# Weight preparation of a fused attention and feed-forward kernel: w3 @ w_out first and whole, lo parts by TensorE and ScalarE, attention queued a slot later

## The chip, the core and the metric

The kernel runs on one core of a Trainium2 chip. A core has five engines with a queue of instructions each: TensorE (PE in the profile; its weight loads are PEld), VectorE (DVE), ScalarE (ACT), GpSimd (POOL) and SyncE (SP, which here only issues DMAs). Matmuls write to PSUM, a memory of eight banks of 128 x 512 fp32; everything else is in SBUF. The metric is the device time of one execution in microseconds; lower is better.

## The reference

Random-feature attention over 8 batches of 576 tokens with 8 heads of 64, and then a bilinear feed-forward block over all 4608 tokens:

```python
def phi(x):                        # 128 random features for each head
    proj = einsum('bhsd,md->bhsm', x, omega)
    h = proj - sum(x * x, -1) / 2
    return exp(h - max(h)) / sqrt(m)
q_p, k_p = phi(q * scale), phi(k * scale)
kv  = einsum('bhsm,bhsd->bhmd', k_p, v);  z = sum(k_p, axis=2)
x   = einsum('bhsm,bhmd->bhsd', q_p, kv) / (einsum('bhsm,bhm->bhs', q_p, z) + 1e-6)
a, b = x @ w1, x @ w2              # x: 4608 x 512, w1 and w2: 512 x 1024
out  = ((a * b) @ w3) @ w_out      # w3: 1024 x 1024, w_out: 1024 x 512
```

q, k, v and omega are fp32, the four weights are float64. The result is fp32.

## The kernel before

**Precision.** An fp32 operand is split into two fp16 parts, hi and lo (x times a power of two s, hi = fp16(x s), lo = x s - hi), and a product is three fp16 matmuls: hi hi, hi lo, lo hi (`PASSES`). `split` (line 132) makes hi on ScalarE and lo on VectorE, with one fused multiply and subtract (lines 136 and 139). `power_of_two` and `pow2` find the scales.

**Weights.** The weights lie in HBM as float64. `from_float64` brings 1 MB at a time into the `arena` as pairs of 32-bit words, by a DMA on ScalarE's queue (`fetch`), takes a magnitude on ScalarE (line 451) and puts the fp32 value together in four VectorE operations (lines 457 to 461). There are three raw buffers. w3 and w_out are never used one by one: the kernel forms W = w3 @ w_out (1024 x 512) with fp32 matmuls and splits that. Here it is done in two halves: two loads of w_out (four of its eight row blocks) and four w3 blocks `W`, whose products give half of every sum; later the other two loads of w_out and four more w3 blocks, whose products VectorE adds to the first (line 537). The fp32 values of w_out and w3 are guests in the second half of `w12b`, where later the second halves of w1 and w2 go. `w12_load` brings a half of w1 or w2, with column sums of the magnitudes by a matmul with ones (line 485), and `w12_split` makes its eight fp16 parts; `W_split` makes those of W and the factors that undo the scales.

**Order of the weights.** `ORDER` is a string of 25 steps: `o` a w_out load, `W` a w3 block, `1` and `2` loads of w1 and w2, `a` and `b` their splits, `S` the split of W. `SKEW` staggers a step's five stages (fetch, magnitude, conversion, nothing, product or magnitudes) over four ticks. `PER` says how many ticks a slot of the main program takes.

**Tokens.** There are 36 chunks of 128 tokens, and three slots of the program for each. The k side runs five chunks ahead of the q side (`LEAD`). `step` puts a chunk's work into slots: sums of squares, scale and split of the raw q and k; in the chunk's first slot `q_chunk` and `k_chunk`, that is projections by 24 matmuls each (`qpj`, `kpj`, line 254), the maximum (line 259), the exponential, and the features' hi and lo parts. A q chunk's features then go through two transposing DMAs on SP's queue (`eqT`, line 344). When a batch's k chunks are done, `kv_batch` forms its kv (line 322). Two slots after `q_chunk` comes `q_attend`: the attention matmuls `nu` (line 357) and the division; one slot after that `ready`: `x_turn` splits x and transposes it by DMA into `xT`.

Two PSUM pools: `ps_a` has two buffers of two banks, shared by qpj, kpj, kv and nu; `ps_m` has four banks for everything else.

**Gates and outputs.** `ready` also appends to a queue the chunk's `gate` units (a, b and their product; for the first four chunks one by one with 96 matmuls of 128 columns each, then in pairs with 48 matmuls of 256 columns) and the `project_out` units (24 matmuls of 512 columns) of the group before. In each slot the program takes one unit from the queue, ahead of the slot's other work; a gate unit waits for the split of its half of w1 and w2, an output for `W_split`. From slot 41 on two units are kept back (`RESERVE`, `EAGER`). What is left at the end is run then.

**Who orders.** The slots give each instruction its priority. A planner that knows the dependences and buffers then writes each engine's order, with its own estimate of when operands are ready: an instruction whose operand it believes late is passed by later ones. At run time each engine keeps that order.

## Time and profile before

| | |
|---|---|
| median of three runs | 932.87 us (929.71 to 1192.34) |
| the profiled execution | 932.87 us, its span 931.1 us |
| mean granted TensorE clock | 0.929 of full speed |
| TensorE busy | 809.9 us (87%) |
| VectorE busy | 637.7 us (68%) |
| ScalarE busy | 406.9 us (44%) |
| GpSimd busy | 324.7 us (35%) |
| DMA | 88.42 MB, mean 95 GB/s |

Times are microseconds from the start of the span unless marked ns. In rows of groups stand the line of the kernel, engine, operation, output <- inputs, shapes and count, then busy time and mean ns of one, then the engine's idle time ahead of them and who ended it. Rows in order of time begin with start and duration; [ ] tells the idle time before and who ended it. An fp32 matmul leaves two records. The rows of stretches give length, then each engine's busy time with its count, the granted TensorE clock, the DMA engines' share and GB/s.

### The profile page before, as it was taken

To read this page: it belongs to the slowest core of one execution; us is meant where nothing else is said; L and a number is where in the kernel's file an instruction comes from. 1 tells how busy PE (TensorE), PEld (TensorE's weight loads), DVE (VectorE), ACT (ScalarE), POOL (GpSimd) and SP (SyncE) were. 2 spreads that over 40 slices of the span, in tenths; PEclk is the share of its full clock that TensorE was granted. 3 is DMA by queue.
4 is the path that set the end of the run, shared out by engine and by line. 5 is a ranking of instruction groups with operands and counts; after the bars stand their busy time and mean duration, and the time that the engine had idled before them with its cause. 6 is when DMAs were issued, how large, how long until landed. Compare 5 with 4: busy or idle time off the path is not lost.

```text
span 931.1 us, 20482 instructions
## 1 busy us (share of the span) xinstructions
PE 809.9 (87%) x8593; PEld 598.3 (64%) x8598; DVE 637.7 (68%) x1119; ACT 406.9 (44%) x695; POOL 324.7 (35%) x317
## 2 busy tenths in 40 slices
PE   1964397689996998999989998989899989999998
PEld 1433253577775766777757766767577757777774
DVE  5779789889787478667876787566857875556210
ACT  3587764556435343444344533444354333322111
POOL 0000004232454256433543464343533643423311
PEclk9985599689998799999989998999899989999999
DMA  8445455332444145333432343243423422333200
GB/s 312 163 137 181 136 148 178 83 70 59 92 114 83 43 91 126 92 70 81 114 80 69 80 125 80 65 96 79 115 71 69 69 59 58 74 76 58 46 24 34
DMA packets 142524, 88.42 MB, mean 95 GB/s; under 512 B 116704, under 2 KB 116832, under 8 KB 142432
## 3 DMA queue, kind: packets, MB, share of 16 engines
q1 hardware_dynamic: 134944, 66.15, 30.1%
q10 hardware_dynamic: 7488, 20.97, 6.7%
q8 instruction: 67, 1.10, 0.5%
q14 instruction: 25, 0.20, 0.1%
HBM read 49.35 MB, written 9.44 MB: 63 GB/s over the span
## 4 chain that ended last, share of the span: by engine, by line
PE 45%; DVE 25%; ACT 11%; DMA 10%; issue 5%; POOL 4%; ACTq 0%; DVEq 0%; SPq 0%; another core or an unknown queue 0%; POOLq 0%
PE ab L581 24%; PE o L607 9%; DVE nm L259 5%; PE kvp L322 4%; PE wp L530 4%; DMA eqT<-eq 3%; DMA qraw<-qT 3%; DVE qhl L139 3%; DVE vhl L139 2%; DVE qe L267 2%; POOL eq L277 2%; PE nu L357 2%; DVE ke L267 2%; ACT ke L268 1%; DMA xT<-xhl 1%
## 5 line engine op out<-in xcount | busy, mean ns | idle before, releaser
L581 PE MATMUL ab<-xT,w12b 128*128 128x256 f16 (+1 forms) x3840 | 408.7, 268 | 12.8 <-DMA xT<-xhl 11.4
L581 PEld LDWEIGHTS <-w12b 128*128 128x128 f16 x3840 | 351.4, 101 | 59.4 <-DMA xT<-xhl 6.8
L607 PE MATMUL o<-Wb,arena 128*128 128x512 f16 x864 | 194.4, 379 | 1.3 <-DVE Wb L139 0.8
L595 POOL TENSOR_SCALAR arena<-asb 128x512 f16<-128x512 f32 x72 | 59.7, 829 | 256.4 <-DVE asb L591 249.5
L607 PEld LDWEIGHTS <-arena 128*128 128x128 f16 x864 | 84.4, 100 | 93.9 <-issue 1.4
L277 POOL TENSOR_TENSOR eq<-qe,eq 128x1024 f16<-128x1024 f32 x34 | 73.3, 2157 | 139.7 <-DVE eq L125 139.7
L268 ACT ACTIVATE qe<-qe,ln_e,es 128x1024 f32<-128x1024 f32 x35 | 43.4, 1240 | 149.5 <-DVE qe L267 149.5
L596 POOL TENSOR_TENSOR arena<-asb,arena 128x512 f16<-128x512 f32 x72 | 92.0, 1277 | 6.0
L139 DVE SCALAR_TENSOR_TENSOR qhl<-qraw,s,qhl 128x512 f16<-128x512 f32 x36 | 68.5, 1904 | 28.6 <-ACT qhl L136 28.5
L591 DVE TENSOR_TENSOR asb<-ab,asb 128x512 f32<-128x512 f32 x72 | 49.5, 688 | 55.3 <-PE ab L581 54.9
L277 POOL TENSOR_TENSOR ek<-ke,ek 128x1024 f16<-128x1024 f32 x28 | 61.5, 2195 | 46.6 <-DVE ek L125 45.3
L153 ACT ACTIVATE junk_q<-qraw 128x512 bf16<-128x512 f32 x36 | 22.7, 631 | 125.2 <-DMA qraw<-qT 125.2
L357 PE MATMUL nu<-kv,eqT 128*128 128x65 f16 (+1 forms) x960 | 40.7, 204 | 40.5 <-DMA eqT<-eq 40.0
L357 PEld LDWEIGHTS <-eqT 128*128 128x128 f16 (+1 forms) x960 | 35.6, 107 | 51.6 <-DMA eqT<-eq 45.2
L530 PE MATMUL wp<-w12b 128*128 128x512 f32 x128 | 62.4, 644 | 4.8 <-DVE w12b L461 4.8
L322 PE MATMUL kvp<-vhl,ek 128*128 128x65 f16 x960 | 50.5, 206 | 11.0 <-POOL ek L277 4.7
L603 DVE TENSOR_SCALAR osc<-pt,kap 128x1 f32<-128x1 f32 x36 | 9.6, 272 | 68.8 <-ACT o L611 68.7
L322 PEld LDWEIGHTS <-ek 128*128 128x128 f16 x960 | 41.4, 104 | 22.4 <-POOL ek L277 4.8
L590 ACT ACTIVATE asb<-ab 128x512 f32<-128x512 f32 x72 | 41.8, 580 | 28.2 <-PE ab L581 28.2
L254 PE MATMUL kpj<-om,khl 64*128 64x128 f16 x864 | 34.0, 226 | 21.5 <-ACT khl L136 17.2
L530 PEld LDWEIGHTS wp<-w12b 128*128 128x128 f32 x128 | 25.7, 206 | 35.6 <-issue 29.9
L393 ACT ACTIVATE xhl<-xs,p2r 128x512 f16<-128x512 f32 x36 | 25.8, 718 | 49.3 <-DVE p2r L182 44.3
(120 smaller groups left out, 1037.5 us busy)
## 6 DMA issues: line engine op xcount, KB each, us to landing
kraw<-kT SPq DMA_DIRECT2D x36, 256.0 KB, 3.0
vraw<-v SPq DMA_DIRECT2D x36, 256.0 KB, 3.0
qraw<-qT SPq DMA_DIRECT2D x36, 256.0 KB, 2.6
out<-o SPq DMA_DIRECT2D x36, 256.0 KB, 2.0
arena<-w3T ACTq DMA_DIRECT2D x8, 1024.0 KB, 5.4
arena<-w ACTq DMA_DIRECT2D x8, 1024.0 KB, 5.9
arena<-wo ACTq DMA_DIRECT2D x4, 1024.0 KB, 5.3
eqT<-eq SPq DMA_TRANSPOSE x72, 3.0
```

The lines of the kernel that those rows point to most:

```text
L139: nc.vector.scalar_tensor_tensor(lo, src, s, hi, ALU.mult, ALU.subtract)
L259: nc.vector.tensor_reduce(nm, pj, AX.X, ALU.max, negate=True)
L268: nc.scalar.activation(e, e, AF.Exp, scale=es, bias=ln_e)
L277: (nc.vector if lo == "d" else nc.gpsimd).tensor_tensor(t[:, 1], e, t[:, 0], ALU.subtract)
L322: nc.tensor.matmul(ps[:, h // 4, h % 4], ek[c][r0:r1, x, place(h)], vhl[c][r0:r1, y, h], start=n == 0, stop=n == len(mm) - 1,)
L357: nc.tensor.matmul(nu[r0:r1, h // 4, h % 4], t[:, x, place(h), r0:r1], kvs[b][:, y, h], start=n == 0, stop=n == 2,)
L530: nc.tensor.matmul(ps, w[:, j, k * P : (k + 1) * P], guest[:, j], start=j == 0, stop=j == HALF - 1)
L581: nc.tensor.matmul(ps[:, k], w12[m][i][cc][:, a, r * P : (r + 1) * P], x[:, b, cc, off : off + T], start=j == 0, stop=j == len(mm) - 1,)
L591: nc.vector.tensor_tensor(asb, ab[1], asb, ALU.mult)
L595: nc.gpsimd.tensor_scalar(h[:, 0], asb, 1.0, 1.0, ALU.mult, ALU.mult)
L596: nc.gpsimd.tensor_tensor(h[:, 1], asb, h[:, 0], ALU.subtract)
L607: nc.tensor.matmul(ps, hs[c, f][0][:, a], W[f][:, b], start=i == 0, stop=i == len(mm) - 1)
```

## The change

Three things change together.

1. All of w3 @ w_out comes first: four w_out loads, then eight w3 blocks, each of which now covers 128 columns of the transposed w3 over all rows of w_out (before: 256 columns over half of them), so that a product is one sum of eight matmuls, copied out by ScalarE; the additions on VectorE are gone. w_out lies in the second half of `w12b`, the w3 blocks in three places of the first half, in which w1 goes afterwards. `ORDER` and `PER` are rewritten: after the first three ticks every slot takes one, so all weights are through at slot 25 instead of 31.
2. The 24 splits of weights use `split_by_pe`: hi on ScalarE as before; then lo is formed in PSUM by an fp32 matmul with a scaled identity (x s) and an fp16 matmul with minus the identity (- hi), and ScalarE copies it out as fp16. The identity is made at the start.
3. From chunk 4 on (`EARLY`), `q_attend` comes three slots after `q_chunk` instead of two, and `ready` four instead of three.

```diff
@@ -40,14 +41,15 @@
 DK = "11111110"
 
 
-ORDER = "ooWWWW11a22booWWWW11a22bS"
+ORDER = "ooooWWWWWWWW11a22b11a22bS"
 SKEW = [0, 1, 2, 2, 3]
 
-PER = [3, 1, 0, 1, 0, 1, 1, 0, 1, 0, 1, 1, 0, 1, 1, 0, 1, 1, 1, 1, 1] + 12 * [1]
+PER = [3] + 20 * [1] + 14 * [1]
 PACE = {}
 GROUPS = [(0, 1), (1, 1), (2, 1), (3, 1)]
 RESERVE = 2
 EAGER = 40
+EARLY = 4
 RAW64_BUFS = 3
 O_BUFS = 3
 RAW_BUFS = 2
@@ -113,6 +115,10 @@
     def small(name, n=1, rows=P, dt=F32, bufs=4):
         return sm.tile([rows, n], dt, tag=f"s_{name}", name=name, bufs=bufs)
 
+    ident = const.tile([P, P], F32, name="ident")
+    make_identity(nc, ident)
+    minus = const.tile([P, P], F16, name="minus")
+    nc.scalar.mul(minus, ident, -1.0)
     ones_bf = const.tile([P, P], BF16, name="ones_bf")
     nc.vector.memset(ones_bf, 1.0)
     ones = const.tile([P, P], F32, name="ones")
@@ -141,6 +147,20 @@
             nc.gpsimd.tensor_scalar(src, src, s, 1.0, ALU.mult, ALU.mult)
             copy(kind == "d", hi, src)
             nc.gpsimd.tensor_tensor(lo, src, hi, ALU.subtract)
+
+    def diagonal(s, name):
+
+        t = sm.tile([P, P], F32, tag="diag", name=f"diag_{name}", bufs=2)
+        nc.scalar.mul(t, ident, s)
+        return t
+
+    def split_by_pe(hi, lo, src, s, d, name):
+
+        nc.scalar.mul(hi, src, s)
+        ps = bank_m(f"lo_{name}")
+        nc.tensor.matmul(ps, d, src, start=True, stop=False)
+        nc.tensor.matmul(ps, minus, hi, start=False, stop=True)
+        nc.scalar.copy(lo, ps)
 
     def square_sum(out, src, name, pre=1.0):
 
@@ -499,46 +519,41 @@
         kaps[n, i] = pow2(l1m, 1, f"w{n}_{i}", bufs=4)
         s = small("ws")
         nc.vector.tensor_scalar_mul(s, kaps[n, i][1], 2.0**12)
+        diag = diagonal(s, f"w{n}_{i}")
         for cc in range(NC):
             d = w12[n][i][cc]
-            split(pick(WS, (i * 2 + n) * NC + cc), d[:, 0], d[:, 1], w12b[:, i, n * NC + cc + 1], s)
-
-
-    HALF = NF // 2
-    guest = w12b[:, 1]
+            name = f"w{n}_{i}_{cc}"
+            split_by_pe(d[:, 0], d[:, 1], w12b[:, i, n * NC + cc + 1], s, diag, name)
+
+
+    guest = w12b.rearrange("p i b f -> p (i b) f")
 
     def wo_load(n):
         j = 2 * n
-        at = j % HALF
+        at = 2 * NC + 2 + j
         dst = guest[:, at : at + 2].rearrange("p j o -> p (j o)")
         src = wo[j * P : (j + 2) * P].rearrange("(j p) o -> p j o", p=P)
         return from_float64(lambda: dst, src, f"wo_{j}")
 
     wam = const.tile([P, NF], F32, name="wam")
 
-    def W_block(n):
-
-        i, j0 = n * 2 % NF, n * 2 // NF * HALF
-        at = HALF + n % 2 * 2
+    def W_block(i):
+
+        at = i % 3 * 2
         w3c = guest[:, at : at + 2].rearrange("p b i -> p (b i)")
 
         def product():
-            w = w3c.rearrange("p (j i) -> p j i", j=HALF)
-            for k in range(2):
-                ps = bank_m(f"wp_{n}_{k}")
-                for j in range(HALF):
-                    nc.tensor.matmul(
-                        ps, w[:, j, k * P : (k + 1) * P], guest[:, j], start=j == 0, stop=j == HALF - 1
-                    )
-                Wi = Wb[:, i + k + 1]
-                if j0 == 0:
-                    nc.scalar.copy(Wi, ps)
-                else:
-                    nc.vector.tensor_tensor(Wi, ps, Wi, ALU.add)
-                    square_sum(wam[:, i + k : i + k + 1], Wi, f"W{i + k}")
-
-        src = w3T[j0 * P : (j0 + HALF) * P, 2 * i * P : 2 * (i + 2) * P]
-        return from_float64(lambda: w3c, src.rearrange("(j p) i -> p j i", p=P), f"w3_{n}") + [product]
+            w = w3c.rearrange("p (j i) -> p j i", j=NF)
+            ps = bank_m(f"wp_{i}")
+            for j in range(NF):
+                nc.tensor.matmul(
+                    ps, w[:, j], guest[:, 2 * NC + 2 + j], start=j == 0, stop=j == NF - 1
+                )
+            nc.scalar.copy(Wb[:, i + 1], ps)
+            square_sum(wam[:, i : i + 1], Wb[:, i + 1], f"W{i}")
+
+        src = w3T[:, 2 * i * P : 2 * (i + 1) * P]
+        return from_float64(lambda: w3c, src.rearrange("(j p) i -> p j i", p=P), f"w3_{i}") + [product]
 
     def W_split():
         p, s = power_of_two(wam, NF, "W", add=True, bufs=1)
@@ -560,8 +575,10 @@
             nc.vector.tensor_scalar(q, q, 1.0, s, ALU.min, ALU.mult)
             ss.append(q)
         done.add("k")
+        ds = [diagonal(q, f"W{i}") for i, q in enumerate(ss)]
         for i in range(NF):
-            split(pick(WS, 4 * NC + i), W[i][:, 0], W[i][:, 1], Wb[:, i + 1], ss[i * 2 // NF])
+            h = i * 2 // NF
+            split_by_pe(W[i][:, 0], W[i][:, 1], Wb[:, i + 1], ss[h], ds[h], f"W{i}")
 
     hs = {}
 
@@ -721,8 +738,9 @@
         put(at0 - 1, 8, splits)
         if i >= 0:
             put(at0, 1, lambda: q_chunk(i))
-            put(at0 + 2, 7, lambda: q_attend(i))
-            put(at0 + 3, 0, lambda: ready(i))
+            lag = 2 if i < EARLY else 3
+            put(at0 + lag, 7, lambda: q_attend(i))
+            put(at0 + lag + 1, 0, lambda: ready(i))
         if kc < NCH:
             put(at0, 2, lambda: k_chunk(kc))
         if kc in B_OF_K:
```

More of the change, by code (lines that the diff above doesn't have):

```diff
@@ L6 @@
 from concourse import mybir
+from concourse.masks import make_identity
 from concourse._compat import with_exitstack
```

## Prediction

> **What bounds the kernel now.** I read the page first, then the busy times cut into stretches at events of the code: start to first w3 product, to the end of the first half of the products (57.64 us), to the first gate, to the projections of query chunk 5 (233.10 us), to the point where the queue of gates stands the same in both kernels, to the end.
>
> ```profile
> span 931.1 us, 20482 instructions
> ...
> PE 809.9 (87%) x8593; PEld 598.3 (64%) x8598; DVE 637.7 (68%) x1119; ACT 406.9 (44%) x695; POOL 324.7 (35%) x317
> ```
> ```profile
> core 0: us, PE busy (x) PEld busy (x) DVE busy (x) ACT busy (x) POOL busy (x), PEclk, DMA share, GB/s
> 0.00:24.44 24.44, 3.40 (x30) 2.62 (x30) 13.69 (x32) 8.49 (x13) 0.66 (x14) 1.00 0.87 317
> 24.44:57.64 33.20, 33.20 (x117) 14.83 (x118) 23.90 (x36) 22.20 (x46) 0.00 (x0) 1.00 0.36 120
> 57.64:134.56 76.92, 38.70 (x338) 23.11 (x339) 66.23 (x116) 55.97 (x111) 0.67 (x8) 0.65 0.55 168
> 134.56:233.10 98.54, 76.81 (x1028) 60.39 (x1030) 88.41 (x165) 54.43 (x97) 30.85 (x30) 0.86 0.38 96
> 233.10:294.00 60.90, 55.77 (x688) 41.87 (x687) 50.04 (x86) 24.89 (x41) 27.03 (x21) 0.94 0.41 100
> 294.00:931.00 637.00, 601.99 (x6402) 455.50 (x6400) 395.41 (x691) 240.97 (x390) 265.47 (x244) 0.97 0.33 76
> ```
> TensorE is the bound as a whole (87%) but not in each stretch. It idles 931.1 - 809.9 = 121 us: 21.0 before the first product, none during the first products, 38.2 and 21.7 in the two stretches in which the weights are still being prepared (VectorE busy 86% and 90%: there VectorE sets the pace, and the clock falls to 0.65), then 5.1 and 35.0 us. So VectorE work is worth something only up to about 233 us, and TensorE work costs its full length wherever TensorE has a backlog. What the idle 35.0 us at the end are, the waits of TensorE in that stretch say, and one of them in order of time:
>
> ```profile
> PE nu L357 <- DMA eqT<-eq: 26.3, 15, 2.7
> PE kvp L322 <- POOL ek L277: 4.7, 1, 4.7
> ```
> ```profile
> 459.02 0.84 PE L254 MATMUL qpj<-om,qhl 64*128 64x128 f16 x24
> 459.70 0.83 PE L254 MATMUL kpj<-om,khl 64*128 64x128 f16 x24
> 460.46 5.42 PE L581 MATMUL ab<-xT,w12b 128*128 128x256 f16 x48
> 465.07 1.21 DVE L259 TENSOR_REDUCE nm<-qpj 128x8 f32<-128x1024 f32 x1
> 465.86 5.34 PE L607 MATMUL o<-Wb,arena 128*128 128x512 f16 x24
> 466.31 1.23 DVE L267 TENSOR_TENSOR qe<-qpj,nm 128x1024 f32<-128x1024 f32 x1
> 473.68 0.24 PE L357 MATMUL nu<-kv,eqT 128*128 128x65 f16 x2 [2.48 <-DMA eqT<-eq]
> 475.85 1.39 PE L357 MATMUL nu<-kv,eqT 128*128 128x65 f16 x22 [1.94 <-DMA eqT<-eq]
> 477.06 7.35 PE L581 MATMUL ab<-xT,w12b 128*128 128x256 f16 x48
> 484.34 0.84 PE L254 MATMUL qpj<-om,qhl 64*128 64x128 f16 x24
> 484.37 1.23 SPq L398 DMA_TRANSPOSE xT<-xhl  x1
> 485.23 1.23 DVE L259 TENSOR_REDUCE nm<-qpj 128x8 f32<-128x1024 f32 x1
> 486.56 1.23 DVE L267 TENSOR_TENSOR qe<-qpj,nm 128x1024 f32<-128x1024 f32 x1
> ```
> The attention of a chunk (nu) waits for its transposed features: 2.48 + 1.94 us here, and the 48 gate matmuls behind it take 7.35 us where 48 others take 5.42: a stall costs some 1.9 us of clock on top. This comes back about every 4.5 chunks, when VectorE is held by the v splits: its first reading of the projections starts 465.07 - 459.86 = 5.2 us after they end; in the next chunk 0.05 us after.
>
> **The change, part by part.** The prices:
>
> ```profile
> 42.53 10.42 PE wp L530 x24
> ```
> ```profile
> L460 DVE SCALAR_TENSOR_TENSOR arena<-arena 128x1024 uint32<-128x1024 uint32 x20 | 26.4, 1319 | 0.2
> L461 DVE SCALAR_TENSOR_TENSOR w12b<-arena 128x1024 uint32<-128x1024 uint32 x20 | 24.9, 1244 | 0.7 <-DVE arena L460 0.5
> L457 DVE TENSOR_SCALAR arena<-arena 128x1024 f32<-128x1024 f32 x20 | 14.8, 740 | 9.5 <-ACT arena L451 9.5
> L459 DVE TENSOR_SCALAR arena<-arena 128x1024 uint32<-128x1024 uint32 x20 | 13.7, 685 | 0.1
> L139 DVE SCALAR_TENSOR_TENSOR w12b<-w12b,ws 128x512 f16<-128x512 f32 x16 | 12.9, 809 | 1.8 <-ACT w12b L136 1.8
> L537 DVE TENSOR_TENSOR Wb<-wp,Wb 128x512 f32<-128x512 f32 x8 | 5.5, 684 | 2.2 <-PE wp L530 2.2
> L535 ACT COPY Wb<-wp 128x512 f32<-128x512 f32 x8 | 4.8, 603 | 7.5 <-PE wp L530 7.4
> ```
> *Lo parts.* An fp32 matmul of 512 columns leaves two records; 24 records in 10.42 us make 0.87 us a matmul. A split adds one of these and one fp16 matmul of 512 columns (5.34 us / 24 = 0.22): 1.09 us of TensorE. 24 splits: 26.2 us. VectorE loses 24 x 0.81 = 19.4 us and the 8 additions of half products, 5.5 us. ScalarE keeps the hi parts and gets 24 copies out of PSUM at 0.60 (14.5 us) and 6 scaled identities, a quarter of the columns, so below 0.60 each. Its copy waits for two matmuls that stand in TensorE's order, and behind it wait the exponentials and the gate copies. The Trainium skill (Perfetto Trace Analysis, Engine Utilization) gives fp32 matmuls half the output rate; read as a whole product this would be an estimated 0.43 us instead of 0.87 and the sum 10.5 us less. The trace shows 0.43 per record and two records, so it doesn't hold here.
>
> *Identity at the start.* One small ScalarE multiply (below 0.60) behind a few GpSimd operations. ScalarE had no data yet in that time (8.49 us busy of the first 24.44), so I take 0; if it stood ahead of the first weight DMA on that queue, the loads would start 1 to 2 us later.
>
> *Order of loads.* All four w_out loads come first, so the first w3 block is the fifth load and no longer the third:
>
> ```profile
> 23.16 1.22 DVE L461 SCALAR_TENSOR_TENSOR w12b<-arena 128x1024 uint32<-128x1024 uint32 x1
> ...
> 28.54 1.22 DVE L461 SCALAR_TENSOR_TENSOR w12b<-arena 128x1024 uint32<-128x1024 uint32 x1
> ```
> The third and fourth loads end 5.4 us apart, so the products start 2 x 5.4 = 10.8 us later, at 35.2 (bounds: 4 us less if the loads run closer, 4 more). Then all 64 matmuls run in one piece: the 33.2 us of the first half and 32 x 0.87 = 27.8 for the other: they end at 96.2, where the first half ended at 57.6. That is +38.6 us, with all products done.
>
> *End of the products to the first gate.* Before: 76.9 us, VectorE busy 66.2, ScalarE 56.0. A load costs VectorE the four rows' 1.32 + 1.24 + 0.74 + 0.69 = 3.99 us. Eight end in this stretch before; after it about five loads' worth are left, since the first w1 loads are converted up to their last operation while TensorE multiplies (that last one must wait: its destination holds w3). VectorE: 66.2 - 12 (loads) - 6.5 (eight lo parts) - 2.7 (four additions) = 45. ScalarE: it loses some 7 us (square sums, conversions), gains 8 to 12 copies, 5 to 7 us, and the waits between; some 56 to 58. So ScalarE and the latency of the first query chunk take VectorE's place; I take 60 us, bounds 50 and 77. First gate at 156 us instead of 134.6: +21.6.
>
> *First gate to the projections of chunk 5.*
>
> ```profile
> 134.56 5.52 PE L581 MATMUL ab<-xT,w12b 128*128 128x128 f16 x96 [1.47 <-DMA xT<-xhl]
> ```
> Before, 98.5 us with seven units of gate or output (one is the row above). The second halves of w1 and w2 are now ready six turns earlier in the queue, so eleven units fit: 8 x 5.52 + 3 x 5.34 = 60; 14 of the splits 15; four pairs of projections at 1.67 and four attentions at up to 1.4 make 12.3; I leave 11 for a kv product and for waits: 98.7. Even, but 21 us of units ahead.
>
> *An empty queue.*
>
> ```profile
> 260.48 5.26 PE ab L581 x48
> ```
> That lead is used up at once: chunks 4 and 5 are attended a slot later, the queue runs dry, and four turns have no unit. From the projections of chunk 5 to the first gate of chunks 4 and 5 lie then feature, transposes, attention and x transposes: 484.4 - 459.0 = 25.4 us to the issue in the delayed chunk above, 5 less without the v splits, 3 more for the landing and 3 for chunk 6's projections ahead of the attention: 26 us, of which TensorE works some 5. Before, the same way (to the row above) took 260.5 - 233.1 = 27.4 us and held the four units. -1.4, together +20.2.
>
> *To 294 us.* Before 5.1 us idle and about 3 at the low clock. Afterwards two units in reserve fill these gaps: -7, together +13.
>
> *The attention a slot later.* The 26.3 us go, as a whole slot (a unit of 5.3 us) now lies between; with them about six times 1.9 us of clock, 11.6, and I give half of the 4.7 us. What is late next is PSUM: projections of q and k and nu share two buffers, and in the new order nu(c) comes right behind the projections of c+1, so it takes the buffer of q's, free when VectorE has read it twice: 0.05 + 1.23 + 1.23 and the gap between, 2.6 us (459.86 to 467.54 = 7.7 in the delayed chunk). Which TensorE work lies in between is written before the run, by a planner:
>
> ```profile
> 224.04 0.39 PE L581 MATMUL ab<-xT,w12b 128*128 128x128 f16 x4
> 224.27 0.38 PE L607 MATMUL o<-Wb,arena 128*128 128x512 f16 x1
> ```
> Gate matmuls stand between those of an output whose operand isn't ready, so the planner will put gate matmuls between the projections and nu, as long as it believes the reading to take. I take 0.25 us of error in 25 chunks and 1 us in the seven delayed ones: 13 us (bounds 0 and 35). -40 + 13 = -27. The x transposes of a chunk move too: on SP's queue they now stand behind the next chunk's two feature transposes and its loads. The two to eight units that the queue holds from here on (10 to 40 us of gates) hide that; without them it would be the 26 us of the empty queue again.
>
> **Sum:** 931.1 + 13 - 27 = 917 us of span. The profiled execution took 932.87, which is also the median, 1.8 above its span: 919; as the waits that I rounded up (of the 11 us and the 13) are more often smaller, I say 917.
>
> **Rivals.**
> *Slower: nu stands straight behind the projections.* Then each of 32 chunks pays the reading less kpj's 0.83 us: 25 x 1.8 + 7 x 6.9 = 93 us in place of 13: about 1000 us. It decides against the change from a mean wait of 1.5 us (951.5 - 917 + 13 = 48 us over 32). For it: this buffer is tight in every chunk and VectorE runs late by up to 5.2 us. Against: the interleaved rows. The Trainium skill (TensorE: Matmul & The Clock Gate, Part 2) says that matmuls run strictly in program order; the fences agree, nu at 473.68 held a ready gate. Chance 0.11.
> *ScalarE takes VectorE's place early:* the stretch to the first gate stays at 77 us, 917 + 17 = 934, no change. For it: ScalarE's 56 us there, against it 45 us of VectorE. Beside it the Trainium skill (ScalarE: Activation LUTs, Rules for kernel authors) sends plain multiplies and additions to VectorE rather than ScalarE; the rows agree only half, 0.81 for the fused subtraction against a copy of 0.60. Chance 0.22.
> *The lag does nothing*, as the planner sets nu just as early: the 27 us stay, 944. Against: a unit more lies ahead of nu in program order. Part of the former chance.
> *All of it works:* 50 us to the first gate, no new waits: 917 - 10 - 13 - 6 = 888. For it: the lists of VectorE there fall by a third. Chance 0.24.
>
> **Numbers.** Forecast 917, chance 0.43, its own span 900 to 932. 2% is about what a measurement of this kernel can tell from no change: 914 and 951.5. Faster: 0.24 and half of the forecast's, 0.45. Same: 0.22 and the other half, 0.44. Slower: 0.11. Range 885 to 945.
>
> **What would show it.** First product at 35 us and first gate near 156; TensorE empty for some 20 us before the first 256-column gate; no eqT wait behind 300 us, nu waiting for VectorE's qe instead, about 13 us in all; TensorE's busy time up by 15 to 20. Wrong if the first gate comes before 146 or behind 170, or if nu waits over 35 us.

## The result, and the profile after

The changed kernel takes 972.99 us (median; 969.31 to 975.82), the kernel before 932.31 us beside it: a ratio of 1.0444, 95% interval [1.0395, 1.0493]. It is slower by 4.4%. One run of the kernel before, far slower at 1192.34 us, counts in that median but not in the ratio. The forecast was 917 us with a range of 885 to 945, so the time lies outside the range and on the other side of no change.

The page of the kernel after, its span and its busy times:

```profile
span 970.8 us, 20614 instructions
...
PE 830.8 (86%) x8665; PEld 602.2 (62%) x8670; DVE 606.3 (62%) x1087; ACT 423.9 (44%) x726; POOL 307.0 (32%) x319
```

TensorE is busy 20.9 us more than before (forecast 15 to 20) and VectorE 31.4 us less (forecast 19.4 + 5.5). But 20.9 us of busy time is about half of the 39.7 us by which the span grew. TensorE also idles more: 970.8 - 830.8 = 140 us instead of 121.

The same kernel by stretches, cut at the events of the forecast's steps (start to first w3 product, to the end of the products, to the first gate, to the projections of chunk 5, to the first gate with 256 columns, to the end); the columns are those of the table of before:

```profile
0.00:32.27 32.27, 3.41 (x31) 2.62 (x31) 22.35 (x45) 12.83 (x24) 1.08 (x16) 1.00 0.88 311
32.27:91.90 59.63, 59.63 (x186) 26.86 (x188) 45.50 (x66) 37.67 (x73) 0.00 (x0) 1.00 0.53 165
91.90:157.56 65.66, 36.76 (x340) 19.92 (x343) 47.07 (x84) 52.80 (x106) 0.59 (x8) 0.77 0.40 119
157.56:264.90 107.34, 94.87 (x1225) 72.55 (x1225) 55.75 (x115) 54.15 (x100) 30.56 (x36) 0.89 0.28 65
264.90:296.01 31.11, 10.71 (x222) 8.81 (x221) 29.03 (x48) 14.23 (x24) 8.82 (x4) 0.60 0.49 94
296.01:970.80 674.79, 625.41 (x6668) 471.48 (x6667) 406.62 (x732) 252.22 (x404) 265.97 (x255) 0.97 0.32 75
```

And the kernel before, cut at its own first gate and its own first gate with 256 columns:

```profile
0.00:134.56 134.56, 75.31 (x481) 40.56 (x484) 103.81 (x181) 86.66 (x170) 1.33 (x22) 0.80 0.56 183
134.56:260.34 125.78, 103.80 (x1397) 80.17 (x1400) 110.20 (x197) 65.84 (x114) 40.95 (x39) 0.89 0.37 92
```

| event, us | before | forecast | after |
|---|---|---|---|
| first product | 24.4 | 35.2 | 32.3 |
| products through | (in two parts) | 96.2 | 91.9 |
| first gate | 134.6 | 156 | 157.6 |
| projections of chunk 5 | 233.1 | 254.7 | 264.9 |
| first gate with 256 columns | 260.3 | 280.7 | 296.0 |
| from there to the end | 670.8 | 636.3 | 674.8 |

The forecast's column is its own sum: 156 + 98.7 = 254.7, + 26 = 280.7, and the rest of 917. The first gate comes within 1.6 us of the forecast, in part by luck: the products ended 4.3 us earlier than forecast and the stretch behind them took 5.7 us longer. Of the 53.8 us by which the forecast misses the span, 1.6 arise up to the first gate, 8.6 and 5.1 in the next two stretches, and 38.5 in the long rest, which was to become 34 us shorter (27 by the lag, 7 by the units in reserve) and is 4 us longer than before.

The waits of TensorE from 300 us on, kernel after:

```profile
PE nu L377 <- DVE qe L287: 32.8, 21, 4.1
PE nu L377 <- DMA vraw<-v: 7.9, 2, 4.1
```

No wait for eqT is left, as forecast; the 26.3 us of before are gone. In their place nu waits 40.7 us for the PSUM buffer of the next chunk's projections. The second row is the same wait: VectorE's qe ended last there too, while the profile names a DMA. In order of time the 23 waits are 16 of 0.8 to 1.3 us (16.2 together), 2 of 2.2, and 5 of 3.7 to 4.1 (20.1 together). The rows of TensorE and VectorE in order of time show one of the large and one of the small ones:

```profile
488.84 5.12 DVE L145 SCALAR_TENSOR_TENSOR vhl<-vraw,s,vhl 128x512 f16<-128x512 f32 x5 [1.93 <-POOL vhl L144]
489.98 0.84 PE L274 MATMUL qpj<-om,qhl 64*128 64x128 f16 x24
490.66 0.83 PE L274 MATMUL kpj<-om,khl 64*128 64x128 f16 x24
491.43 1.26 PE L598 MATMUL ab<-xT,w12b 128*128 128x256 f16 x10
494.07 1.20 DVE L279 TENSOR_REDUCE nm<-qpj 128x8 f32<-128x1024 f32 x1
495.31 1.22 DVE L287 TENSOR_TENSOR qe<-qpj,nm 128x1024 f32<-128x1024 f32 x1
496.68 1.48 PE L377 MATMUL nu<-kv,eqT 128*128 128x65 f16 x24 [3.99 <-DVE qe L287]
497.97 5.36 PE L598 MATMUL ab<-xT,w12b 128*128 128x256 f16 x38
...
539.53 0.84 PE L274 MATMUL qpj<-om,qhl 64*128 64x128 f16 x24
540.21 0.83 PE L274 MATMUL kpj<-om,khl 64*128 64x128 f16 x24
540.54 1.21 DVE L279 TENSOR_REDUCE nm<-qpj 128x8 f32<-128x1024 f32 x1
540.97 1.27 PE L598 MATMUL ab<-xT,w12b 128*128 128x256 f16 x10
541.86 1.23 DVE L287 TENSOR_TENSOR qe<-qpj,nm 128x1024 f32<-128x1024 f32 x1
543.23 0.89 PE L377 MATMUL nu<-kv,eqT 128*128 128x65 f16 x24 [0.99 <-DVE qe L287]
```

In the lower chunk, which has no delay, VectorE reads the projections without loss: from their end (540.37) to the end of qe (543.09) it takes 2.72 us. TensorE has kpj and ten gate matmuls for that time, up to 542.24, and then 0.99 us of nothing. In the upper chunk VectorE is at the v splits until 493.96 and the reading ends at 496.53; again only ten gate matmuls stand ahead of nu, and TensorE loses 3.99 us although 38 more gate matmuls of the same unit stand behind it. The Trainium skill (TensorE: Matmul & The Clock Gate, Part 2) says that matmuls are issued in program order; these rows agree, the 38 run at 497.97, behind nu.

### The profile page after: what moved, and what is told of

Its sections match the earlier page's. It is cut to its first block, busy times and chain, and to the rows that moved or that the text cites. A ratio compares the mean times of both kernels' runs of the same rounds, so it can differ in the third digit from the quotient of the medians.

```text
span 970.8 us, 20614 instructions
## 1 busy us (share of the span) xinstructions
PE 830.8 (86%) x8665; PEld 602.2 (62%) x8670; DVE 606.3 (62%) x1087; ACT 423.9 (44%) x726; POOL 307.0 (32%) x319
## 4 chain that ended last, share of the span: by engine, by line
PE 57%; DVE 21%; ACT 10%; DMA 5%; issue 5%; POOL 2%; SPq 0%; DVEq 0%; another core or an unknown queue 0%; POOLq 0%; ACTq 0%
PE ab L598 27%; PE o L624 13%; PE wp L549 6%; PE kvp L342 4%; DVE nm L279 3%; DVE qe L287 3%; DVE vhl L145 3%; PE nu L377 2%; DVE xhl L414 2%; ACT o L628 1%; ACT ke L285 1%; DMA qraw<-qT 1%; ACT qe L288 1%; PE lo_w L161 1%; DVE ke L287 1%
## 5 line engine op out<-in xcount | busy, mean ns | idle before, releaser
L598 PEld LDWEIGHTS <-w12b 128*128 128x128 f16 x3840 | 346.9, 100 | 50.0 <-issue 7.9
L612 POOL TENSOR_SCALAR arena<-asb 128x512 f16<-128x512 f32 x72 | 54.1, 751 | 144.7 <-DVE asb L608 92.0
L613 POOL TENSOR_TENSOR arena<-asb,arena 128x512 f16<-128x512 f32 x72 | 83.9, 1165 | 6.0
L377 PEld LDWEIGHTS <-eqT 128*128 128x128 f16 (+1 forms) x960 | 33.3, 106 | 60.9 <-issue 32.5
L414 DVE SCALAR_TENSOR_TENSOR xhl<-xs,p2r,xhl 128x512 f16<-128x512 f32 x36 | 61.6, 1710 | 11.1 <-ACT xhl L413 10.4
L628 ACT ACTIVATE o<-o,osc 128x512 f32<-128x512 f32 x36 | 24.6, 684 | 92.4 <-PE o L624 92.4
L549 PE MATMUL wp<-w12b 128*128 128x512 f32 x128 | 58.2, 612 | 5.6 <-DVE w12b L481 5.6
L142 ACT ACTIVATE qhl<-qraw,s 128x512 f16<-128x512 f32 x36 | 26.0, 722 | 80.2 <-DVE s L193 79.2
L279 DVE TENSOR_REDUCE nm<-qpj 128x8 f32<-128x1024 f32 x36 | 43.7, 1215 | 10.8 <-PE qpj L274 10.8
L145 DVE SCALAR_TENSOR_TENSOR qhl<-qraw,s,qhl 128x512 f16<-128x512 f32 x36 | 37.4, 1038 | 20.2 <-ACT qhl L142 20.2
L342 PE MATMUL kvp<-vhl,ek 128*128 128x65 f16 x960 | 46.7, 200 | 3.5 <-ACT ek L133 2.2
```

The source lines that it names most:

```text
L145: nc.vector.scalar_tensor_tensor(lo, src, s, hi, ALU.mult, ALU.subtract)
L279: nc.vector.tensor_reduce(nm, pj, AX.X, ALU.max, negate=True)
L342: nc.tensor.matmul(ps[:, h // 4, h % 4], ek[c][r0:r1, x, place(h)], vhl[c][r0:r1, y, h], start=n == 0, stop=n == len(mm) - 1,)
L377: nc.tensor.matmul(nu[r0:r1, h // 4, h % 4], t[:, x, place(h), r0:r1], kvs[b][:, y, h], start=n == 0, stop=n == 2,)
L414: nc.vector.scalar_tensor_tensor(t[:, 1], xs, r, t[:, 0], ALU.mult, ALU.subtract)
L549: nc.tensor.matmul(ps, w[:, j], guest[:, 2 * NC + 2 + j], start=j == 0, stop=j == NF - 1)
```

## The experiments

All ratios are against the kernel before on the same chip, with their 95% interval. That kernel took 935.12 us beside e1 to e4 and 932.1 to 932.5 us beside the others, so across these two sets the ratios are compared and not the times. The expectations and the text name the runs by their labels, e1 to e14.

### Which part costs it

**The lag alone (e1).** The kernel before, with the attention a slot later from chunk 4 on:

```diff
-            put(at0 + 2, 7, lambda: q_attend(i))
-            put(at0 + 3, 0, lambda: ready(i))
+            lag = 2 if i < EARLY else 3
+            put(at0 + lag, 7, lambda: q_attend(i))
+            put(at0 + lag + 1, 0, lambda: ready(i))
```

> The kernel before with only the later attention (three slots from chunk 4 on). Theory A, the attention now waits for the PSUM buffer of the next chunk's q projections instead of for its transposes, about as long: 931 to 942 us, the waits of nu on eqT nearly gone and some 35 to 40 us on qe in their place. Theory B, the lag is worth the 27 us that I gave it and all of the loss lies in the weights: 900 to 910. Theory C, the lag is the loss: 960 or more.

Measured: 949.23 us, 1.0133 [1.0080, 1.0186]. The waits of TensorE from 300 us on:

```profile
PE nu L358 <- DVE qe L268: 27.8, 19, 4.1
PE nu L358 <- DMA vraw<-v: 11.6, 3, 4.1
```

39.4 us, with the same sizes chunk by chunk as in the whole change (about 1.0 in a chunk without delay, 3.7 to 4.1 in a delayed one). The waits are those of theory A, the time lies above its interval and in none of the three. The span of the profiled execution (949.8 us) is 18.7 us longer than before; only 10.7 of that lie in the rest behind the first gate with 256 columns, and 8.0 ahead of it, where the gate comes at 268.4 instead of 260.3 us. So the lag brings a loss with it also when nothing is done to the weights. The part that was to gain 27 us and more costs some 14 (949.23 - 935.12).

**The whole change without the lag (e2):**

```diff
-EARLY = 4
+EARLY = 99
```

> The changed kernel with the attention left two slots behind for all chunks. Theory A: 960 to 970 us (4 us of waits and one slot of the empty queue less than 973). Theory B: 995 to 1005. Theory C: 930 to 940.

Measured: 965.89 us, 1.0330 [1.0311, 1.0349], as theory A has it. The waits from 300 us on, and the stretches to its first gate and to its first gate with 256 columns:

```profile
PE nu L377 <- DMA eqT<-eq: 30.4, 17, 3.9
```
```profile
0.00:160.20 160.20, 103.06 (x553) 50.63 (x558) 114.95 (x193) 103.25 (x202) 1.68 (x24) 0.88 0.54 173
160.20:293.94 133.74, 102.64 (x1398) 78.97 (x1399) 78.38 (x153) 65.32 (x116) 39.86 (x40) 0.85 0.30 69
```

The waits for eqT are back, the waits of nu for qe are gone, and the kernel is 7 us faster than the whole change by the times, 11 by the ratios. The rest behind the first gate with 256 columns takes 672.3 us, 2.5 less than in the whole change. So the lag accounts for a part of the 4.4% only; the work on the weights costs 3.3% by itself.

**The lo parts alone (e3).** The kernel before with `split_by_pe` for its 24 weight splits, order and lag as before:

```diff
-            split(pick(WS, (i * 2 + n) * NC + cc), d[:, 0], d[:, 1], w12b[:, i, n * NC + cc + 1], s)
...
+            split_by_pe(d[:, 0], d[:, 1], w12b[:, i, n * NC + cc + 1], s, diag, name)
...
-            split(pick(WS, 4 * NC + i), W[i][:, 0], W[i][:, 1], Wb[:, i + 1], ss[i * 2 // NF])
...
+            split_by_pe(W[i][:, 0], W[i][:, 1], Wb[:, i + 1], ss[h], ds[h], f"W{i}")
```

> The kernel before with only the lo parts made by TensorE and ScalarE. Theory A, 26 us of matmuls and more with their waits lie on TensorE's path and VectorE's 19 us are worth less: 942 to 955 us. Rival, VectorE sets the pace of the weights' stage and its 19 us are worth their length: 912 to 925.

Measured: 948.08 us, 1.0131 [1.0102, 1.0159]. The stretches to its first gate and to its first gate with 256 columns:

```profile
0.00:138.06 138.06, 85.15 (x504) 44.15 (x507) 98.11 (x171) 89.12 (x175) 1.74 (x24) 0.83 0.55 178
138.06:277.42 139.36, 119.33 (x1446) 86.29 (x1449) 100.14 (x183) 76.48 (x140) 40.16 (x39) 0.89 0.33 84
```

TensorE is busy 85.15 + 119.33 = 204.5 us there, 25.4 more than in the kernel before (75.31 + 103.80 = 179.1), and the first gate with 256 columns comes 17.1 us later. Ahead of the first gate TensorE gets 9.8 us more and the gate comes 3.5 us later: most is hidden. Behind it TensorE gets 15.5 us more and the stretch is 13.6 us longer: hardly anything is. VectorE's 16 us less in the two stretches buy nothing that shows: theory A.

**The new order alone (e4).** The kernel before with the new `ORDER`, `W_block`, `wo_load` and `PER`; splits as before, no lag:

```diff
-ORDER = "ooWWWW11a22booWWWW11a22bS"
+ORDER = "ooooWWWWWWWW11a22b11a22bS"
...
-PER = [3, 1, 0, 1, 0, 1, 1, 0, 1, 0, 1, 1, 0, 1, 1, 0, 1, 1, 1, 1, 1] + 12 * [1]
+PER = [3] + 20 * [1] + 14 * [1]
```

> The kernel before with only the new order of loads and products (w_out and w3 first, whole sums), the old splits on VectorE and the attention two slots behind. Theory A, the queue of gates runs dry once and the first gate comes some 20 us later, which is only partly made good by the products done: 940 to 955 us. Rival, the order itself is a gain (TensorE busy without a gap for 60 us, 5.5 us of additions saved) and the loss is all in the split: 915 to 930.

Measured: 952.24 us, 1.0180 [1.0154, 1.0206].

```profile
0.00:157.03 157.03, 86.84 (x518) 46.11 (x522) 117.81 (x200) 96.30 (x187) 1.74 (x24) 0.83 0.55 176
157.03:275.70 118.67, 87.91 (x1362) 72.98 (x1363) 93.17 (x170) 59.01 (x101) 41.31 (x40) 0.86 0.35 78
```

Here TensorE has even less to do ahead of the first gate with 256 columns (174.8 us), and idles 101 us instead of 81; the time is in theory A's interval. The three parts alone cost 1.3, 1.3 and 1.8%: their sum is the 4.4% of the whole. Added one after another (e4, e2, the whole change) they cost 1.8, 1.5 and 1.1%, the same within the intervals. The runs on the pace, below, show that this holds for the new table of ticks only.

### What the lag loses, and why

**nu ahead of the gates (e5).** If the planner's gates between the projections and nu were the matter, nu could be put ahead of the projections of its slot (the edit is against e1):

```diff
-            put(at0 + lag, 7, lambda: q_attend(i))
+            put(at0 + lag, 7 if i < EARLY else 0.5, lambda: q_attend(i))
```

> The kernel before with the later attention, but put ahead of the next chunk's projections instead of behind them. If the lag fails because nu takes the PSUM buffer that the projections just ahead of it have filled (theory A), nu now finds a free buffer and transposes that landed a unit ago: waits of nu in the long stretch (40 us in e1) below 10, now and then 1 us of kpj waiting for nu's reading instead, 905 to 922 us. If the later place itself costs (theory C: x, its transposes and the gates a slot later), 940 to 950 as in e1.

Measured: 951.51 us, 1.0218 [1.0189, 1.0247]. Its waits from 300 us on:

```profile
PE kpj L255 <- DVE xs L373: 35.2, 22, 4.5
```

The waits of nu for qe are gone, and the next user of the same buffers waits instead: the projection of k needs the buffer that nu has just filled, and waits until VectorE has read it (xs). 35.2 us in 22 waits, and no time is won; the time lies just above the interval of theory C, but what theory A says of the buffer is what the waits show. The wait belongs to the pair of buffers and not to nu.

**nu in banks of its own (e6).** From chunk 4 on nu goes to two of the four banks of the other pool, and VectorE reads them one at a time:

```diff
-        nu = banks(f"nu_{c}")[:, :, 0 : 4 * E].rearrange("p g (i e) -> p g i e", e=E)
...
+            nus = [
+                bank_m(f"nu_{c}_{g}")[:, 0 : 4 * E].rearrange("p (i e) -> p i e", e=E) for g in range(2)
+            ]
...
```

> The kernel before with the later attention behind the projections as in e1, but from chunk 4 on nu lies in two of the four single banks instead of the shared double ones (its sums are then read in two halves, four VectorE operations instead of two). Theory A: no wait of nu on qe, 910 to 930 us, the more the less the gates miss these banks. Theory C: 940 to 955.

Measured: 935.73 us, 1.0036 [1.0021, 1.0051]; faster than the lag with shared buffers by 13.5 us, or by 9 by the ratios. The time lies between the two theories. From the start to the end all waits of nu for qe are gone; of the waits that came in their place the largest is

```profile
PE norm_q_k L159 <- DVE xs L379: 20.4, 9, 3.6
```

The wait of 1.0 us in each chunk without delay has gone: these chunks again follow each other every 18.2 to 18.5 us, where the whole change takes 19.1 to 19.4 and the kernel before 18.1 to 18.8. This shows that the shared buffers cost that wait. In the delayed chunks a wait of up to 3.6 us has stayed and moved to the banks of the other pool. The rest behind the first gate with 256 columns takes 933.9 - 265.27 = 668.6 us against 670.8 before, so that a lag without its buffer conflict wins about 2 us, if anything, of the 26.3 us of waits that it removes: executions of one kernel differ by more than that. The first gate with 256 columns comes 5 us later (265.3 instead of 260.3), which is more than it wins.

### The pace

**The new order at the old pace (e8).** The order alone, as above, with the old table of ticks for a slot (`PER` of before):

```diff
-PER = [3] + 20 * [1] + 14 * [1]
+PER = [3, 1, 0, 1, 0, 1, 1, 0, 1, 0, 1, 1, 0, 1, 1, 0, 1, 1, 1, 1, 1] + 12 * [1]
```

> e4 (new order of loads and products alone) with the old pace of 28 ticks over 32 slots. If e4 lost because the w3 products, the only long TensorE work there is before the gates, were used up in one piece and left nothing to fill the gaps of the first chunks (theory A), spreading them lowers TensorE's idle time before the first gate by 10 us or more, and the first gate comes before 150 us; the time 935 to 948, as the second halves come later again. If it lost by the later first product and the guests' places alone, it stays at 950 to 958.

Measured: 932.47 us, 1.0005 [0.9985, 1.0024].

```profile
0.00:140.44 140.44, 83.50 (x516) 43.18 (x519) 103.07 (x177) 91.18 (x185) 1.68 (x24) 0.89 0.55 178
140.44:263.78 123.34, 94.26 (x1362) 76.13 (x1366) 105.08 (x194) 61.53 (x100) 39.90 (x39) 0.83 0.38 91
```

All of the order's 1.8% is due to the table. With the old one the first gate comes at 140.4 instead of 157.0 us. VectorE is busy 103.1 us up to there instead of 117.8: with one tick in every slot, more of the weights' work stands ahead of the first gate, which needs only the first halves of w1 and w2. The first gate and TensorE's idle time ahead of it (56.9 us instead of 70.2) are as theory A has them; the time is below its interval.

**The whole change at the old pace (e12)**, by the same two lines:

```diff
-PER = [3] + 20 * [1] + 14 * [1]
+PER = [3, 1, 0, 1, 0, 1, 1, 0, 1, 0, 1, 1, 0, 1, 1, 0, 1, 1, 1, 1, 1] + 12 * [1]
```

> The whole change with the old table of ticks per slot (PER as before); order of the weights, lo parts by TensorE and the lag stay. Theory: the pace alone is what the new order lost (its run with the old table took as long as the kernel before, the one with the new table 1.8% longer), and the parts of the change add up: the time falls from 973 to 948 to 960 us, 1.5 to 3% above the kernel before, the first gate comes near 140 us instead of 157.6. Rival: in the whole change the pace costs nothing of its own, since TensorE's lo parts and not VectorE's list now fill the stretch: 965 to 975 us, with the first gate earlier and the wait ahead of the first 256-column gate longer by as much.

Measured: 969.52 us, 1.0393 [1.0332, 1.0454]. The theory named there fails: only 3.5 us come back, which the intervals don't tell from nothing (the whole change has 1.0395 to 1.0493), and the first gate comes at 154.5 us in spite of the old table. The time is the rival's; but the first gate with 256 columns comes earlier too (290.4 us instead of 296.0), which the rival did not expect. So parts that add up when each is tried alone need not add up when one is taken out of the whole.

**The new order at the old pace, with the lo parts, without the lag (e14)**, that is the edit above and one more:

```diff
-EARLY = 4
+EARLY = 99
```

> The new order at the old pace (old table of ticks) with the lo parts by TensorE and ScalarE, without the lag (attention two slots after the projections throughout). Apart, the new order at the old pace cost nothing (932.5) and the lo parts 1.3%. Theory, the two get in each other's way, because the new order puts all splits where ScalarE's exponentials of the first chunks are: 952 to 960 us, the first gate near 154 us as in the whole change at the old pace, instead of 138 to 140 in each of the two alone. Rival, it is the lag that adds more than its own 1.3% once the queue is shorter: 940 to 948 us, and the first gate near 154 us costs nothing in the end.

Measured: 952.79 us, 1.0213 [1.0170, 1.0255].

```profile
0.00:155.09 155.09, 99.56 (x570) 50.00 (x573) 113.19 (x201) 100.95 (x203) 9.76 (x30) 0.89 0.55 173
155.09:285.03 129.94, 104.57 (x1380) 78.75 (x1383) 77.52 (x145) 65.15 (x112) 30.51 (x33) 0.88 0.34 72
```

This completes a ledger of what each kernel takes above the kernel before:

| | old splits | lo parts by TensorE | and the lag |
|---|---|---|---|
| old order, old table | 0 | 1.3% (e3) | not run |
| new order, old table | 0.05% (e8) | 2.1% (e14) | 3.9% (e12) |
| new order, new table | 1.8% (e4) | 3.3% (e2) | 4.4% (the change) |

The new table costs 1.8% with the old splits, 1.2% with the lo parts, and with the lag 0.5%, which is within the noise. The lo parts cost 1.3% in the old order, 2.1% in the new one at the old table and 1.5% at the new table. So they and the order get in each other's way by 0.8% at the old table, where the time and the first gate are those of the theory (155 us, where the lo parts alone have it at 138 and the order alone at 140); at the new table, that of the change, this isn't seen. The lag costs 1.3% alone, 1.8% at the old table and 1.1% at the new one; the intervals don't tell these apart, so the rival's share isn't shown.

The count behind the lo parts is plain. Up to the first gate with 256 columns TensorE is busy 99.56 + 104.57 = 204.1 us, and 83.50 + 94.26 = 177.8 us in e8, which has the same order and table and the old splits. 26.3 us of work are added, that gate comes 21.3 us later (285.03 instead of 263.78), and TensorE's idle time ahead of it falls only from 86.0 to 80.9 us. At the new table (e2 against e4) 30.9 us are added and the gate comes 18.2 us later; in the old order (e3) it is 25.4 and 17.1. So most of what is added to TensorE delays that gate, and 5 to 13 us are hidden.

### The lo parts

**Only the first halves by TensorE (e7).** The lo parts of a and b for the first halves of w1 and w2 (8 of the 24 splits) as in the change, the other 16 as before:

```diff
...
+            if i == 0:
+                split_by_pe(d[:, 0], d[:, 1], w12b[:, i, n * NC + cc + 1], s, diag, name)
+            else:
+                split("a", d[:, 0], d[:, 1], w12b[:, i, n * NC + cc + 1], s)
...
```

> The kernel before with only the eight lo parts of the first halves of w1 and w2 by TensorE and ScalarE (ahead of the first gate, where TensorE idles); the other sixteen as before. If TensorE time costs only where there is a backlog of gates (theory A), no loss: 926 to 934 us. If the back and forth between ScalarE and TensorE costs wherever it stands (rival), a third of e3's 13 us or more: 936 to 942.

Measured: 935.57 us, 1.0034 [1.0017, 1.0052]. The time lies between the two intervals. A third of the splits costs 3.3 us, with an interval of 1.6 to 4.8, and all of them cost 13.0: this is not told from a third. These eight lie ahead of the first gate, where TensorE has idle time; yet even there they win nothing.

**Copied out by VectorE (e13).** The whole change, with one word of `split_by_pe` exchanged:

```diff
-        nc.scalar.copy(lo, ps)
+        nc.vector.tensor_copy(lo, ps)
```

> The whole change, but the lo parts that TensorE forms in PSUM are copied out by VectorE instead of ScalarE (24 copies). In the profile after, the chain of waits between the end of the products and the first gate lies mostly on ScalarE (exponentials of k and q chunks, hi and lo parts of w1 and w2 in turn). Theory, ScalarE's list sets the first gate there: the first gate comes 4 to 8 us before 157.6 us and the time falls to 962 to 968. Rival, the list of loads and chunks as a whole sets it and the copies only lie beside it: first gate within 3 us of 157.6, time 968 to 976; VectorE's busy time rises by some 14 us in both.

Measured: 966.18 us, 1.0359 [1.0317, 1.0401].

```profile
0.00:159.21 159.21, 101.17 (x553) 50.76 (x557) 119.94 (x201) 101.74 (x197) 1.68 (x24) 0.88 0.54 174
```

The first gate comes no earlier (159.2 against 157.6), so ScalarE's copies aren't what sets it, although the chain of waits lies mostly on ScalarE there. On the place the rival holds; the time lies in the theory's interval all the same, since 6.8 us are won (the intervals of the two just touch), but behind the first gate and not ahead of it, which neither had foreseen. A copy takes 0.69 us on VectorE in place of 0.58 us on ScalarE.

### The delayed chunks

Every fourth or fifth chunk is delayed because VectorE is at the lo parts of the v splits. `VS` says who splits v; in batches behind the first GpSimd makes hi and VectorE lo.

**All of v by GpSimd (e9)** (kernel before, no other change):

```diff
-VS = "aaaaam"
+VS = "aaaaap"
```

> The kernel before with nothing but the v splits (batches 1 to 7) taken off VectorE: GpSimd scales in place and forms the lo part, ScalarE casts the hi part. Theory D, the wait that comes back every 4.5 chunks is VectorE being late by the burst of five v splits, and the lag only hands it from the transposes to the next thing that needs VectorE: the seven long waits of nu shrink by more than half without any lag, 900 to 920 us. Rival, GpSimd's 95 us more make the feature's lo part as late as VectorE did: 930 to 945.

Measured: 927.08 us, 0.9942 [0.9917, 0.9967]. Its waits from 300 us on, and rows of GpSimd, VectorE and TensorE in order of time:

```profile
PE nu L357 <- DMA eqT<-eq: 25.7, 14, 4.3
```
```profile
736.80 6.03 POOL L143 TENSOR_TENSOR vhl<-vraw,vhl 64x512 f16<-64x512 f32 x5
744.62 2.57 POOL L277 TENSOR_TENSOR eq<-qe,eq 128x1024 f16<-128x1024 f32 x1
745.13 2.60 DVE L139 SCALAR_TENSOR_TENSOR khl<-kraw,s,khl 128x512 f16<-128x512 f32 x1
750.30 0.90 PE L357 MATMUL nu<-kv,eqT 128*128 128x65 f16 x13 [4.30 <-DMA eqT<-eq]
```

VectorE is no longer late: in all 27 chunks behind 300 us it begins to read at most 1.4 us after the end of q's projections (up to 5.4 before). The waits for eqT are as long as before nevertheless. Now GpSimd, which makes the features' lo part (`eq`, line 277), is late by the v splits and two operations of a gate (1.8 us) behind them, and the transpose behind it too. The mechanism is the rival's: the delay has changed its engine and kept its size. The time lies between the two intervals.

**The same with the lag and nu's own banks (e10)**, that is the edits of both:

```diff
-VS = "aaaaam"
+VS = "aaaaap"
...
+            nus = [
+                bank_m(f"nu_{c}_{g}")[:, 0 : 4 * E].rearrange("p (i e) -> p i e", e=E) for g in range(2)
+            ]
...
+            lag = 2 if i < EARLY else 3
```

> e6 (later attention with its own banks) with the v splits off VectorE as in e9. Theory D: nothing is left to wait for in the long stretch, rest after the first 256-column gate below 650 us (668.6 in e6), 905 to 918. If e6's remaining waits (20 us of a norm's bank on nu's reading) are of the banks and not of a late VectorE, they stay: 930 to 938.

Measured: 948.90 us, 1.0177 [1.0139, 1.0215]. Slower than either edit alone (927.08 and 935.73) and above both intervals; from 300 us on norm_q_k still waits 22.6 us for xs, and the gates wait 8.4 us for ScalarE. Why the two don't go together was not found.

**hi of v by ScalarE (e11)** (kernel before):

```diff
-VS = "aaaaam"
+VS = "a"
```

> The kernel before with the hi parts of all v splits on ScalarE instead of GpSimd; VectorE keeps the lo parts. Theory D with GpSimd's share: the five lo parts take 0.75 us instead of 1.18 when GpSimd is not busy beside them, VectorE is late by 2 us less in seven chunks: 915 to 927 us. Rival, only the number of VectorE operations counts: 928 to 937.

Measured: 924.74 us, 0.9924 [0.9898, 0.9949]. This is the fastest of all, 0.8% below the kernel before and 5% below the change, and in theory D's interval. Its waits from 300 us on:

```profile
PE nu L357 <- DMA eqT<-eq: 23.5, 16, 2.8
```

The mechanism is only in part the theory's. In the delayed chunks VectorE begins to read 3.9 to 4.6 us after the projections (before 4.6 to 5.4), but ends as late (7.4 to 8.1 us, before 7.1 to 7.8), and the waits are only some 3 us shorter. GpSimd is relieved (289.6 us busy instead of 324.7).

## Why the prediction was wrong

**What failed: "the attention a slot later", -27 us.** Its mechanism was named rightly: nu takes the buffer of the next q projections, nu then waits for qe, the eqT waits vanish. The sizes were wrong at both ends: the rest was to become 34 us shorter and became 4 us longer. The lag by itself makes it 2.5 us (the change against e2) to 10.7 us (e1) longer.

- The new wait was priced at 13 us, from 0.25 us of the planner's error in 25 chunks and 1 us in seven. It is 40.7 us, above the upper bound of 35: 1.0 us in 16 chunks, 2.2 in two, 4.0 in five. That these are waits for the buffer is shown by e6, in which nu has banks of its own and they are gone. The 0.25 had no row behind it. The rows of before held what was needed for more: from the end of q's projections, the reading takes at least 2.5 us, and kpj, which ends 0.7 us after them, covers that much; the rest must be filled by gates whose number is fixed before the run. It is filled with ten gate matmuls, 1.27 us, in 22 of the 23 chunks, with and without delay alike. That is 27.7 us of the miss.
- The gain of clock, 11.6 us and about 2 of the reserve's 7, was taken as if the stalls vanished. Stalls of a larger sum took their place, and TensorE's busy time in the rest fell by 5.3 us only (1.7 of that are a pair of projections that now stands ahead of the cut). That is 8 us of the miss.
- The other idle time of the rest was to fall by 7.4 us (5.1 ahead of 294 us and 2.3 of the kv product's wait). It fell by 5.0: from 40.0 - 26.3 = 13.7 to 49.4 - 40.7 = 8.7 us. That is the other 2 us of the 38.5.

The weights were forecast wrongly too. Without the lag's -27 the forecast's own sum is 944 us, and the change without the lag (e2) takes 965.89. Its first gate with 256 columns comes at 293.9 us where 280.7 was forecast, and the rest, which the reserve was to make 7 us shorter, is 672.3 us against 670.8 before. The paragraphs below on the lo parts, on the stretch behind the first gate and on the empty queue go through these terms.

The condition for the rival "nu stands straight behind the projections", a mean wait of 1.5 us over 32 chunks, was nearly met: 40.7 / 32 = 1.3. But its mechanism isn't what happened, since gates do stand in between. What happened lies between the forecast and that rival.

**The lo parts, 26.2 us.** The busy time of TensorE in the two products of a split, in the stretches from the end of the products to the first gate and from there to the projections of chunk 5 (kernel after; first the lo parts of w1 and w2, then those of W):

```profile
91.90:157.56 65.66, 17.99 (x36) 5.38 (x24) 7.03 (x12) 0.77 0.40 119
157.56:264.90 107.34, 7.43 (x12) 2.23 (x8) 2.27 (x4) 0.89 0.28 65
...
157.56:264.90 107.34, 10.71 (x24) 3.35 (x16) 4.54 (x8) 0.89 0.28 65
```

The columns behind the length are TensorE, its weight loads and ScalarE's copies of these tiles. 36.1 us for 24 splits are 1.5 us each instead of 1.09. The two prices came from rows of unbroken work (24 records in 10.42 us); here a split is alone between other things and the clock is at 0.77 and 0.89. Yet the busy time that the splits add up to the first gate with 256 columns is 25.4 us in the old order and 26.3 in the new one at the old table, as priced; the mean clock there is a little higher with them (0.86 instead of 0.84, and 0.89 instead of 0.86). By the runs, the larger error is where they were put: the prediction let ten of them (10.9 us) lie in idle time ahead of the first gate and counted 14 (15 us) behind it, in a stretch whose sum left 11 us for waits and a kv product, where TensorE had idled 21.7. TensorE's idle time ahead of the first gate with 256 columns falls with the lo parts by 8.3 us in the old order (81.2 to 72.9), by 5.1 in the new one at the old table and by 12.7 at the new table: most of the added work found no idle time to lie in.

**First gate to the projections of chunk 5: "even", 98.7 us.** It took 107.3. The eleven units were there as forecast (8 gates and 3 outputs, 61.9 us instead of 60), but 12 splits cost 18.1 us where 14 were to cost 15, TensorE idled 12.5 us, and a kv product took 5.4, where 11 had been left for both.

**An empty queue: 26 us.** 31.1 us, with TensorE busy for 10.7 of them; the forecast of some 20 us without work is right (20.4).

**What held.** The first product (32.3 against 35.2), the end of the products (91.9 against 96.2), the end of the products to the first gate (65.7 us against 60, within 50 to 77), the first gate (157.6 against 156), TensorE's busy time (+20.9 against 15 to 20). The identity at the start cost nothing that the first product shows (32.3 us, and 32.5 in e4, which has none). The 60 us stood on VectorE's shorter lists, and the early stretches on VectorE setting the pace. That premise is not borne out: e3 takes the lo parts off VectorE and its first gate comes 3.5 us later, in e14 14.7 us later than in e8. e13 says that ScalarE's copies alone don't set this stretch either.

**The rivals.** "ScalarE takes VectorE's place early" does not have the size: 65.7 us and not 77. ScalarE is the busiest of the five engines there (52.8 us, VectorE 47.1), and VectorE in place of ScalarE for the copies left the first gate where it was; whether ScalarE's list as a whole sets it was not tested. "The lag does nothing" has the wrong cause (the planner did set nu later), yet as a size it was nearest in the rest: 0 against the +2.5 us by which the change is there above e2. Of "all of it works" neither the 50 us nor the lag without new waits came.

## What stays open

Why about 4 us of wait stay in each delayed chunk, whichever engine or buffer is relieved, wasn't settled. The runs show that it moves (eqT, then qe, xs at kpj, xs at norm_q_k, and eqT by way of GpSimd). A likely reason is that the planner packs each engine's order as tightly as its own estimates allow, so that any delay that it doesn't foresee stalls whatever it has put next; no run tested the planner's estimates themselves. Open, too, is which instruction's order makes the new table of ticks cost 1.8% with the old splits, 1.2% with the new ones and, with the lag, nothing clear of noise.

## What to carry to other kernels

Before an operation is moved a slot later, list who else uses its buffer in the new order and how long the buffer is held: a wait for data that is moved past the next user of the same PSUM buffer comes back as a wait for the buffer, in every round and not only in the late ones. Idle time of TensorE in a stretch is no place to put work, unless the idle pieces themselves are seen to be there when that work is ready; here 25 to 31 us of work were added to 81 to 101 us of idle time, and the stretch became 17 to 21 us longer. And parts that sum up when tried alone say little about taking one out of the whole: try both ways.

## What the runs showed of the hardware

A VectorE operation with two operands beside a GpSimd operation can take more than three times its own duration. The lo part of a 128x512 k in the kernel after, at a moment when GpSimd had been idle for 1.90 us until 486.27:

```profile
484.85 0.74 DVE L145 SCALAR_TENSOR_TENSOR khl<-kraw,s,khl 128x512 f16<-128x512 f32 x1
...
486.27 0.62 POOL L612 TENSOR_SCALAR arena<-asb 128x512 f16<-128x512 f32 x1 [1.90 <-DVE vam L317]
```

The same operation takes 2.60 us in the row at 745.13 above (e9), beside a GpSimd operation from 744.62 to 747.19, and ends 0.54 us behind that. This is no single case: in the traces of all runs, 478 such operations of 128x512 began while GpSimd had more than 0.3 us left of a feature's lo part (`eq`, `ek`). They took 0.87 to 2.62 us, and every one ended 0.54 to 0.55 us behind the end of that GpSimd operation. The Trainium skill (SBUF — State Buffer, Who interferes with whom) says that the two engines share a pair of ports by an exclusive lock; the rows agree, as they look like a block until the other's end and not like a shared rate.
